# Block-causal attention with a gated linear unit on one core: the gated unit and its weights four steps later, output weights loaded over all partitions, the output tile ahead of the third score tile, fewer dummy matmuls

## The chip, the cores and the metric

The kernel runs on one core of a Trainium2 chip. The metric is the device time of one execution in microseconds (us). Every ratio below is the mean time of one kernel's fast runs over the mean of the other's fast runs of the same rounds, with a 95% interval; it is therefore not quite the ratio of the medians that stand beside it. A run is called slow when it is over 1.5% above the fastest of the same kernel; slow runs are left out of the ratios.

## The reference

Batch 8, 8 heads, 576 positions, head size 64; all inputs and outputs are float32.

```
scores = 0.125 * q @ k^T, masked so that block i (64 positions) sees blocks j <= i
x      = softmax(scores) @ v, heads side by side: [8, 576, 512]
gate   = sigmoid(causal depthwise convolution of x over 5 positions)
out    = (gate * (x @ w_val)) @ w_out
```

## The kernel before

A *step* handles one pair of heads: p = 0 to 31, four steps per batch element. The *gated unit* follows some steps behind. Its work for a quarter of a batch element, called a gated step here, is half a convolution (one of 80 small matmuls serves two gated steps), two value tiles and about one output tile. The engines are PE (matmuls), ACT (exp, tanh, copies), DVE (copies and products out of the matmul banks) and POOL (casts and masks); SP issues the loads. In the steps traced below each engine's instructions stand in the order in which the program emits them (after the change ACT's copy of the output tile starts at 119.84 us, the third exp, emitted behind it, at 120.32).

```python
# PSUM: two "S" tiles of two banks, used in turn; four "G" banks, used in turn.
psS = tile_pool(name="psS", bufs=2, ...)
GT  = [psG.tile([128, 512], fp32, ...) for i in range(4)]

def s_tile(p, t): ...      # matmuls into the next S tile, then exp on ACT out of it
def s_last(b): ...         # the last 64 positions' keys: the next S tile, then exp
def conv(b, hf): ...       # 80 matmuls into the next S tile and two G banks, then tanh x3 on ACT
def val(b, hf, x): ...     # 4 matmuls into a G bank, then DVE (needs the tanh)
def out_tile(u, t): ...    # 4 matmuls into a G bank, then a copy on ACT, then the store

wr = gbank()
for _ in range(9):                                   # dummy matmuls
    mm(wr[0:128, 0:512], wz[0:128, 0:128], wz[0:128])
cast_qk(0, first=True); trans(0)

def load_w_out(j):                                   # four loads, steps 3 and 4
    nc.sync.dma_start(
        out=w_st2[32 * j:32 * j + 32],
        in_=moe_w_out[128 * j:128 * j + 128].rearrange("(x a) n -> a x n", x=4))

for p in range(NP):
    loads(p)                       # QK tile of step p+4, V tile of step p+2, weights in steps 1 to 4
    s_tile(p, 0); s_tile(p, 1)
    weights(p)
    av(p - 1)
    trans(p + 2)                   # (from step 4 on; needs POOL's cast of that QK tile)
    s_tile(p, 2)
    mask(p); cast_v(p + 1); cast_qk(p + 3)           # POOL; the mask needs the third exp
    bq, m = divmod(p - 5, 4)
    if bq >= 0 and m % 2 == 0: conv(bq, m // 2)
    if p % 4 == 3: s_last((p + 1) // 4)
    xtrans(p - 1)
    out()
    if bq >= 0:
        for x in (0, 1): val(bq, m // 2, 2 * (m % 2) + x)
# ... cut: after the loop, five gated steps without attention work
```

`s_tile` computes scores and their exp, `av` multiplies them with V, `trans` and `xtrans` are transposes on PE (of Q and K, and of the attention's result x), `mask` and the casts to 16 bits run on POOL.

The softmax here doesn't subtract the row's maximum and nothing guards it: scores larger than these inputs give would overflow.

## Time and profile before

| | before |
|---|---|
| median of 4 runs, us | 206.47 (205.06 to 208.52) |
| span of the profiled run, us | 203.2 |
| PE busy | 183.9 us, 91% |
| ACT, DVE, POOL busy | 69%, 64%, 40% |

First the page of the kernel before: busy time by engine, then the span in 40 slices of 5.1 us (busy tenths of PE, granted clock in tenths, DMA busy tenths, GB/s). The granted clock is the share of its full clock that PE was allowed.

```profile
PE 183.9 (91%) x3681; PEld 128.5 (63%) x3681; DVE 129.1 (64%) x283; ACT 140.1 (69%) x190; POOL 82.0 (40%) x168
PE   3789867978999999999999999999999999889992
PEclk9966996699999999999999999999999999999999
DMA  5999999999496769686888769794888542113334
GB/s 148 260 266 292 296 283 180 198 240 236 119 279 184 221 194 269 196 228 174 234 231 233 216 192 264 228 243 114 234 254 247 161 118 85 58 56 108 135 129 155
```

PE looks busy from 50 us on and has holes and a lowered clock before. GB/s falls to 180 and 198 in the seventh and eighth slice, 30 to 41 us, while the DMA share stays at 9 tenths or more.

The same by stretches. The columns are the stretch and its length, then busy us and instruction counts of PE, its weight loads, DVE, ACT and POOL, then granted clock, DMA share (1.0 is 16 engines busy; it is above 1 where more than 16 packets overlap) and GB/s.

```profile
25.00:30.00 5.00, 3.69 (x79) 2.70 (x75) 3.65 (x8) 4.49 (x6) 3.10 (x6) 1.00 1.13 288
30.00:35.00 5.00, 3.91 (x59) 2.89 (x59) 4.36 (x11) 2.96 (x3) 1.41 (x5) 0.75 1.20 176
35.00:40.00 5.00, 4.02 (x107) 3.04 (x108) 2.15 (x3) 2.02 (x4) 1.48 (x3) 0.57 1.17 204
80.00:160.00 80.00, 78.62 (x1743) 56.19 (x1740) 56.17 (x122) 64.35 (x88) 35.59 (x68) 1.00 0.78 220
```

Up to about 50 us the loads set the pace: the DMA engines are full (share 1.13 to 1.20), PE is busy 3.7 to 4.0 of 5 us, and part of that at a lowered clock (0.75 and 0.57). From 80 to 160 us PE is busy 98% of the time and nothing else is.

The chain of waits says the same for the first part (start, duration, what):

```profile
24.41 7.29 DMA qks<-in_k_dram
31.71 8.15 DMA qks<-in_k_dram
39.87 6.47 DMA vs<-in_v_dram
46.78 0.60 POOL v L131
```

Now one steady step in the order of time (start, duration, engine, line, operation, operands). It begins with the first two score tiles at 111.20 us.

```profile
111.20 0.61 PE L33 MATMUL S<-qkT 64*128 64x512 f16 x6
111.41 1.05 POOL L126 CAST qk<-qks 128x1024 f16<-128x1024 f32 x1
111.69 3.04 ACT L185 ACTIVATE pt<-S 128x1024 f16<-128x1024 f32 x3 [0.78 <-PE S L33]
112.66 0.61 PE L151 MATMUL G<-ident,qk 128*128 128x128 f16 x8
113.21 0.28 PE L33 MATMUL S<-qkT 64*128 64x256 f16 x2
```

The three exps run without a gap (3.04 us). The POOL cast that the QK transposes need ends at 112.46, and the transposes start at 112.66: 0.2 us of slack. A step with a convolution takes about 5.7 to 6.0 us and one without 4.84.

### The profile page before, as it was taken

How to read it: one execution, taken by the hardware profiler on the slowest of the kernel's cores; microseconds unless marked ns; L12 is line 12 of the kernel's file. 1: busy time of each engine (PE TensorE's matmuls, PEld its weight loads, DVE VectorE, ACT ScalarE, POOL GpSimd, SP SyncE). 2: the span in 40 equal slices, each digit the busy share in tenths (PEclk: the TensorE clock that was granted, in tenths of full speed). 3: DMA queues.
4: the chain of work that ended last, by engine and by line, in shares of the span. 5: the costliest groups of instructions: out<-in, count | busy, mean ns of one | idle time of the engine just before them, and what ended most of it. 6: DMA issues, size and time to landing. Idle time of an engine off the chain costs nothing.

```text
span 203.2 us, 8654 instructions
## 1 busy us (share of the span) xinstructions
PE 183.9 (91%) x3681; PEld 128.5 (63%) x3681; DVE 129.1 (64%) x283; ACT 140.1 (69%) x190; POOL 82.0 (40%) x168
## 2 busy tenths in 40 slices
PE   3789867978999999999999999999999999889992
PEld 1367655656677676676676766676777766566650
DVE  4237878477576857686768576585768575536251
ACT  4165885457778787878787978778787878692621
POOL 7352953166445454545343534245454542210000
PEclk9966996699999999999999999999999999999999
DMA  5999999999496769686888769794888542113334
GB/s 148 260 266 292 296 283 180 198 240 236 119 279 184 221 194 269 196 228 174 234 231 233 216 192 264 228 243 114 234 254 247 161 118 85 58 56 108 135 129 155
DMA packets 70225, 40.43 MB, mean 199 GB/s; under 512 B 48165, under 2 KB 64549, under 8 KB 70186
## 3 DMA queue, kind: packets, MB, share of 16 engines
q1 hardware_dynamic: 69904, 39.60, 73.8%
q8 instruction: 29, 0.48, 1.1%
q10 hardware_dynamic: 282, 0.27, 0.4%
q14 instruction: 10, 0.08, 0.2%
HBM read 30.42 MB, written 9.44 MB: 196 GB/s over the span
## 4 chain that ended last, share of the span: by engine, by line
PE 59%; ACT 14%; DMA 11%; issue 7%; DVE 5%; POOL 2%; SPq 0%; ACTq 0%; POOLq 0%; DVEq 0%
PE G L33 39%; ACT pt L185 14%; PE S L33 11%; DMA qks<-in_k_dram 8%; PE G L241 5%; DMA vs<-in_v_dram 3%; PE G L151 3%; DVE x L232 3%; DVE rc L231 1%; POOL qk L126 1%; PE G L138 1%; DVE idfold L308 1%; DVE qk L157 0%; DVE osb L289 0%; DVE ident L303 0%
## 5 line engine op out<-in xcount | busy, mean ns | idle before, releaser
L185 ACT ACTIVATE pt<-S 128x1024 f16<-128x1024 f32 x96 | 94.2, 1022 | 35.6 <-PE S L33 33.6
L201 POOL MEMSET pt<- 64x384 f16 x32 | 13.2, 413 | 88.3 <-ACT pt L185 88.3
L277 DVE SCALAR_TENSOR_TENSOR gv<-th,G 128x288 f16<-128x288 f32 x64 | 28.4, 454 | 26.1 <-PE G L33 24.8
L162 DVE COPY qkT<-G 128x1024 f16<-128x1024 f16 x31 | 37.7, 1216 | 5.1 <-PE G L151 5.1
L33 PEld LDWEIGHTS <-pt 128*128 128x128 f16 x960 | 32.5, 100 | 7.3 <-issue 3.8
L33 PE MATMUL G<-xt,w_val 128*128 128x288 f16 x256 | 36.6, 286 | 0.0
L33 PE MATMUL G<-w_out,gv 128*128 128x512 f16 x144 | 36.5, 379 | 0.0
L33 PE MATMUL G<-v,pt 128*128 128x65 f16 x896 | 35.4, 197 | 0.2
L126 POOL CAST qk<-qks 128x1024 f16<-128x1024 f32 x31 | 32.4, 1045 | 3.4 <-DMA qks<-in_k_dram 3.3
L232 DVE TENSOR_TENSOR x<-G,rc 128x320 f16<-128x320 f32 x64 | 31.5, 492 | 2.2
L33 PEld LDWEIGHTS <-w_val 128*128 128x128 f16 x256 | 25.0, 98 | 11.8 <-issue 0.2
L291 ACT COPY osb<-G 128x512 f32<-128x512 f32 x34 | 20.0, 589 | 14.4 <-PE G L33 13.2
L33 PE MATMUL S<-qkT 64*128 64x512 f16 (+1 forms) x248 | 28.7, 308 | 0.3 <-ACT pt L185 0.2
L151 PE MATMUL G<-ident,qk 128*128 128x128 f16 x256 | 21.3, 231 | 5.3 <-POOL qk L126 5.3
L33 PEld LDWEIGHTS <-qkT 64*128 64x128 f16 x496 | 15.3, 95 | 14.7 <-issue 7.7
L231 DVE RECIPROCAL rc<-G 128x5 f32<-128x5 f32 x64 | 12.1, 189 | 16.9 <-PE G L33 16.5
L131 POOL CAST v<-vs 128x512 f16<-128x512 f32 x32 | 19.8, 618 | 5.8 <-DMA vs<-in_v_dram 4.4
L151 PEld LDWEIGHTS <-qk 128*128 128x128 f16 x256 | 16.2, 103 | 6.8 <-POOL qk L126 6.1
L243 DVE COPY xt<-G 128x576 f16<-128x576 f16 x32 | 14.5, 452 | 8.9 <-PE G L241 8.9
L33 PEld LDWEIGHTS <-gv 128*128 128x128 f16 x144 | 12.7, 98 | 10.1 <-DVE gv L277 0.5
L33 PE MATMUL S<-xt,DG 32*32 32x288 f16 x640 | 17.0, 295 | 1.3 <-ACT pt L185 0.5
L33 PE MATMUL G<-xt,DG 32*32 32x288 f16 x640 | 17.1, 296 | 0.0
(53 smaller groups left out, 141.7 us busy)
## 6 DMA issues: line engine op xcount, KB each, us to landing
out_dram<-osb SPq DMA_DIRECT2D x36, 256.0 KB, 2.2
qks<-in_q_dram SPq DMA_DIRECT2D x32, 256.0 KB, 4.2
vs<-in_v_dram SPq DMA_DIRECT2D x64, 128.0 KB, 4.4
qks<-in_k_dram SPq DMA_DIRECT2D x31, 256.0 KB, 4.6
tlst<-in_q_dram SPq DMA_DIRECT2D x8, 128.0 KB, 4.0
tlst<-in_k_dram SPq DMA_DIRECT2D x8, 128.0 KB, 4.6
vtst<-in_v_dram SPq DMA_DIRECT2D x8, 128.0 KB, 5.0
w_st<-in_moe_w_val_dram SPq DMA_DIRECT2D x2, 512.0 KB, 6.9
```

The source lines that it names most:

```text
L33: nc.tensor.matmul(out=out, lhsT=lhsT, rhs=rhs, start=start, stop=stop, skip_group_check=True)
L126: nc.gpsimd.tensor_copy(out=o, in_=s)
L131: nc.gpsimd.tensor_copy(out=v16s[p % NV][0:128, 0:4, 0:2, 0:64], in_=s)
L151: nc.tensor.transpose(out=r[:, o:o + 128], in_=t[0:128, c, 2 * i:2 * i + 2, 0:64], identity=ident16[0:128, 0:128])
L162: nc.vector.tensor_copy(out=o[0:128].rearrange("p i (s n) -> p i s n", n=4), in_=src)
L185: nc.scalar.activation(out=pts[p % NPT][0:128, 0:2, 512 * t:512 * t + 512], in_=s[0:128, 0:2, 0:512], func=AF.Exp, bias=0.0, scale=0.125)
L201: nc.gpsimd.memset(pt[64:128, 0:2, 0:1536].rearrange("p h (t s) -> p h t s", t=3)[:, :, :, 0:64], 0.0)
L231: nc.vector.reciprocal(out=rc[0:128], in_=O[:, :, 64:65])
L232: nc.vector.tensor_tensor(out=x[0:128, 0:5, h, 0:64], in0=O[:, :, 0:64], in1=rc[0:128].to_broadcast([128, 5, 64]), op=ALU.mult)
L243: nc.vector.tensor_copy(out=xts[b % NX][0:128, g, 4:4 + SEQ], in_=r[:, 0:SEQ])
L277: nc.vector.scalar_tensor_tensor(out=gv[u][0:128, x, bi, hf, 0:288], in0=t[0:128, x, 0:288], scalar=1.0, in1=r[0:128, 0:288], op0=ALU.add, ...
L291: nc.scalar.copy(out=o[0:128], in_=r[0:128, 0:512])
```

## The change

The intent: the loads of 2 MB of weights shall not compete with the loads of the first steps, so they and the gated unit come four steps later (the lag grows from five steps to nine); the output weights shall spread over all 128 partitions; fewer dummy matmuls stand ahead of the first real work; and the output tile gives PE something to do ahead of the third score tile.

The diff, cut to its core:

```diff
-    for _ in range(9):
-        mm(wr[0:128, 0:512], wz[0:128, 0:128], wz[0:128])
+    warm(4)
     cast_qk(0, first=True)
     trans(0)
+    warm(3)
...
-    def load_w_out(j):
+    def load_w_out(x):
         nc.sync.dma_start(
-            out=w_st2[32 * j:32 * j + 32],
-            in_=moe_w_out[128 * j:128 * j + 128].rearrange("(x a) n -> a x n", x=4))
+            out=w_st2[0:128, x],
+            in_=moe_w_out.rearrange("(j x a) n -> x j a n", j=4, x=4)[x])
... (value weights: loaded in steps 4, 5 for 1, 2; scaled in 7 to 10 for 4 to 6;
...  output weights: loaded in steps 6, 7 for 3, 4; cast in 9, 10 for 6, 7)
     for p in range(NP):
+        gs = p - 9
         loads(p); s_tile(p, 0); s_tile(p, 1); weights(p); av(p - 1)
         trans(p + 2)                      # from gs >= 0 on; at the end of the step before that
+        out()
+        if len(outs) > 2: out()
         s_tile(p, 2)
         mask(p); cast_v(p + 1); cast_qk(p + 3)
-        conv(...)                         # when due
         if p % 4 == 3: s_last((p + 1) // 4)
+        if gs >= 0 and gs % 2 == 0: conv(gs // 4, gs % 4 // 2)
         xtrans(p - 1)
-        out()
-        if len(outs) > 2: out()
         val(...), val(...)
... (after the loop nine gated steps for five; in the last two batch elements DVE copies every second output tile)
```

More of the change, by code (lines that the diff above doesn't have):

```diff
@@ L287, in out_tile @@
         o = p4.tile([128, 512], fp32, tag="osb", name="osb")
-        if u == B // 2 - 1 and t >= 6 and t % 2 == 0:
+        if u == B // 2 - 1 and t % 2 == 0:
             nc.vector.tensor_copy(out=o[0:128], in_=r[0:128, 0:512])
@@ L328, with warm @@
     wr = gbank()
-    for _ in range(9):
-        mm(wr[0:128, 0:512], wz[0:128, 0:128], wz[0:128])
+    def warm(n):
+        for _ in range(n):
+            mm(wr[0:128, 0:512], wz[0:128, 0:128], wz[0:128])
+    warm(4)
     cast_qk(0, first=True)
     trans(0)
+    warm(3)
     cast_tails(0, nc.vector)
@@ L366, in weights @@
                                     in1=convT[0:128].to_broadcast([128, 20, 32]), op=ALU.mult)
-        for x in {4: (0,), 5: (1,), 6: (2, 3)}.get(s, ()):
+        for x in {7: (0,), 8: (1,), 9: (2,), 10: (3,)}.get(s, ()):
             nc.vector.tensor_scalar(
@@ L372, in weights @@
                 scalar1=0.5, scalar2=None, op0=ALU.mult)
-        if s in (6, 7):
-            a = 2 * (s - 6)
+        if s in (9, 10):
+            a = 2 * (s - 9)
             nc.gpsimd.tensor_copy(out=w_out_sb[0:128, a:a + 2, 0:512],
@@ L387, in loads @@
             load_vtail(b + 1)
-        if p in (1, 2):
-            load_w_val(p - 1)
-        if p in (3, 4):
-            load_w_out(2 * p - 6)
-            load_w_out(2 * p - 5)
+        if p in (4, 5):
+            load_w_val(p - 4)
+        if p in (6, 7):
+            load_w_out(2 * p - 12)
+            load_w_out(2 * p - 11)
     outs = []
@@ L402, in out @@
             out_tile(*outs.pop(0))
+    LAG = 9
     for p in range(NP):
+        gs = p - LAG
         loads(p)
@@ L411 @@
             av(p - 1)
-        if 3 < p < NP - 2:
+        if gs >= 0 and p + 2 < NP:
             trans(p + 2)
@@ L415 @@
                 trans_tails((p + 2) // 4)
+        out()
+        if len(outs) > 2:
+            out()
         if p > 0:
@@ L426 @@
                 cast_tails((p + 3) // 4, nc.gpsimd)
-        if p < 4:
+        if p % 4 == 3 and p + 1 < NP:
+            s_last((p + 1) // 4)
+        if gs >= 0 and gs % 2 == 0:
+            conv(gs // 4, gs % 4 // 2)
+        if p > 0:
+            xtrans(p - 1)
+        if gs < 0:
             trans(p + 2)
@@ L430 @@
                 trans_tails((p + 2) // 4)
-        bq, m = divmod(p - 5, 4)
-        if bq >= 0 and m % 2 == 0:
-            conv(bq, m // 2)
-        if p % 4 == 3 and p + 1 < NP:
-            s_last((p + 1) // 4)
-        if p > 0:
-            xtrans(p - 1)
-        out()
-        if len(outs) > 2:
-            out()
-        if bq >= 0:
-            for x in (0, 1):
-                val(bq, m // 2, 2 * (m % 2) + x)
-            if m % 2 == 1:
-                complete(bq, m // 2)
-    b = B - 1
-    av(NP - 1)
-    out()
-    for x in (2, 3):
-        val(b - 1, 1, x)
-    complete(b - 1, 1)
-    xtrans(NP - 1)
-    out()
-    conv(b, 0)
-    out()
-    conv(b, 1)
-    out()
-    for hf in range(2):
-        for x in range(4):
-            val(b, hf, x)
-            out()
-        complete(b, hf)
+        else:
+            for x in (0, 1):
+                val(gs // 4, gs % 4 // 2, 2 * (gs % 2) + x)
+            if gs % 2 == 1:
+                complete(gs // 4, gs % 4 // 2)
+    av(NP - 1)
+    for gs in range(NP - LAG, NP):
+        b, hf = gs // 4, gs % 4 // 2
+        for x in (0, 1):
+            out()
+            val(b, hf, 2 * (gs % 2) + x)
+        if gs == NP - LAG:
+            xtrans(NP - 1)
+        if gs % 2 == 1:
+            complete(b, hf)
+            if gs + 1 < NP:
+                conv((gs + 1) // 4, (gs + 1) % 4 // 2)
     while outs:
```

## The prediction

> **What bounds the kernel now.** Two regimes. (a) To about 53 us the loads bound it: the chain of waits holds 22 us of landing loads between 24.4 and 46.3 us, the table by stretches shows PE busy only 3.6 to 4.4 of each 5 us with granted clock 0.57 to 0.75 in 30 to 40 us, and the DMA share is 1.1 to 1.2. Rate drops from about 290 to 180-200 GB/s at 30-41 us, when the four output-weight loads (256 KB each into 32 partitions, 7.5 to 9 us to landing) are in flight. [...] (b) From step 8 (53.1 us) PE bounds it: 98% busy; the 24 steps to 182.7 us take 5.40 us each (timeline: scores 0+1 0.54, AV 0.92, transposes 0.55, third scores 0.33, gated unit 2.6). The tail is dense too.
>
> **Early gains.** With four dummies, the first transposes start near 5.2 instead of 7.3 us: 2 us. Without weights in steps 1 to 4 [...], loads run at about 3.05 us per step (landings before), and step 10 starts near 50 us with 10 attention steps and one gated step done, against step 8 at 53.1 with three gated steps. A gated step costs PE about what an attention step costs (2.6 and 2.75 us), so the net gain is 4 to 6 us.
>
> **Steady losses.** In the trace exp of the third tile ends 3.5-3.75 us after a step's start. Ahead of it now stand the output matmuls (0.87) and their ACT copy (copy starts 1.07 after the first matmul, takes 0.5-0.6). So it ends near 4.6. Three things hang on it:
> 1. POOL: mask, V cast, QK cast follow that exp in 2.2 us plus 0.1; the next step's QK transposes wait for that cast and have only 0.2-0.4 us of slack. After the short (even) step they wait about 0.6-0.7 us, every second step.
> 2. Score ring of two buffers: in steps 11, 15, 19, 23, 27 the tail-score tile now precedes the conv, so conv takes the third tile's buffer and waits for its exp: about 1.1 us.
> 3. G ring of four banks: the second val tile reuses conv's first G bank, whose tanh follows exp: 0.2-0.4 us, as the output tile no longer stands between conv and val.
> Sum about 2.5-2.9 us per four steps beyond step 10, 12-15 us in all.
>
> **Sum.** 203.2 - 5 + 13 = 211 us of span; the timed run was 2.4 us over the span: 213.5 us, range 205 to 220. Faster by over 2%: 0.08; within 2%: 0.17; slower: 0.75.
>
> **What would show it.** First score matmul near 7.7 us instead of 9.8. DMA rate without the 180 GB/s trough. Gated step 0 starting near 45-48 us. PE busy share in 80-160 us down from 98% to about 87%; waits of the QK transposes on the POOL cast (none there now) in odd steps; score/conv matmuls waiting for the exp in every fourth step; val waiting for tanh. Steps near 6.0 us instead of 5.4.
>
> **What would make it wrong.** If the exp isn't delayed, the early gain wins: 199-202 us. [...]

I expected the output-weight loads to be faster over all partitions. The sum came to 203.2 - 5 + 13 = 211 us of span and 213.5 us of time: the 5 is the middle of the 4 to 6 us of early gain, an estimate of mine, and that these loads would be faster came from no trace.

## The result, and the profile after

| | before | after |
|---|---|---|
| median of 4 runs, us | 206.47 (205.06 to 208.52) | 227.14 (226.42 to 228.07) |
| ratio of the fast runs | | 1.103 (1.094 to 1.112) |
| span of the profiled run, us | 203.2 | 225.1 |
| PE busy | 91% | 83% |

The change makes the kernel 10.3% slower. I had predicted 3.8% slower (213.5 us) and a range that ends at 220. The direction was right, the size was not.

The page of the kernel after:

```profile
PE 186.4 (83%) x3679; PEld 126.5 (56%) x3679; DVE 132.5 (59%) x286; ACT 136.2 (60%) x187; POOL 82.9 (37%) x168
PE   3868977594377989878997989698987989999993
PEclk9959999769958999999999999999999999999999
DMA  5999989935894767666766667676773311134333
GB/s 156 273 266 285 215 232 337 219 107 156 211 262 128 210 188 210 188 189 190 209 174 162 193 196 199 195 185 191 238 204 106 93 50 49 49 119 157 115 134 143
```

The trough of 180 GB/s hasn't gone: it has moved to 45 to 56 us and deepened to 107 and 156 GB/s, and now the DMA share falls with it (3 and 5 tenths). The DMA engines are largely idle there (share 0.40 and 0.48). By stretches:

```profile
40.00:45.00 5.00, 2.94 (x31) 1.94 (x31) 3.19 (x7) 2.02 (x4) 1.84 (x4) 0.67 1.02 210
45.00:50.00 5.00, 4.72 (x82) 3.97 (x80) 3.82 (x8) 3.27 (x4) 2.37 (x5) 0.65 0.40 111
50.00:55.00 5.00, 1.94 (x100) 1.56 (x96) 2.51 (x7) 1.69 (x3) 2.58 (x3) 1.00 0.48 132
80.00:160.00 80.00, 70.43 (x1522) 47.76 (x1520) 50.18 (x108) 55.02 (x77) 32.03 (x61) 1.00 0.68 194
```

PE is busy 88% in the stretch where it was 98%. The chain of waits in the early part, and SP's issues there:

```profile
43.09 8.55 DMA vs<-in_v_dram
54.16 1.84 SPq L83
56.56 4.97 DMA vs<-in_v_dram
```

```profile
44.71 5.16 SPq L364 DMA_DIRECT2D w_st<-in_moe_w_out_dram  x2
49.91 0.87 SPq L92 DMA_DIRECT2D tlst<-in_q_dram  x1
51.56 2.56 SPq L83 DMA_DIRECT2D qks<-in_q_dram  x1
```

A V load that was issued at 43.09 landed 8.6 us later. That time alone shows little: in the kernel before, the V load between the two pairs of output-weight loads (issued at 34.19) took 7.61 us, and a K load 8.15 us. What is new is that SP was held 5.16 us by the issue of two output-weight loads, one of them 3.70 us (with the old form at the same place, in run e1 below, the longest took 1.94 us).

How many packets were in flight at each full microsecond, counted from the packet records of the two traces:

```
before, 30 to 42 us: 16 18 19 21 19 21 17 17 16 18 19 16 17
after,  44 to 56 us: 18  9 11  4  4  4  4  4 14 14  4 12 11
```

Four at each of five full microseconds. That number was the first lead. (The trace doesn't name the engine of a packet. The DMA share from 47 to 51 us is 0.27; four of 16 engines would be 0.25.)

A steady step after the change, the one that begins at 116.09 us (first score tiles at 116.09, then as shown):

```profile
117.22 1.05 POOL L126 CAST qk<-qks 128x1024 f16<-128x1024 f32 x1
118.32 0.62 PE L151 MATMUL G<-ident,qk 128*128 128x128 f16 x8 [0.59 <-POOL qk L126]
118.78 1.03 PE L33 MATMUL G<-w_out,gv 128*128 128x512 f16 x4
119.73 0.28 PE L33 MATMUL S<-qkT 64*128 64x256 f16 x2
119.84 0.58 ACT L291 COPY osb<-G 128x512 f32<-128x512 f32 x1 [1.31 <-PE G L33]
120.32 1.03 ACT L185 ACTIVATE pt<-S 128x1024 f16<-128x1024 f32 x1
121.40 0.29 PE L33 MATMUL S<-xt,DG 32*32 32x288 f16 x2 [1.15 <-ACT pt L185]
```

The bracket is the idle time of the engine before the instruction and what ended it. The third exp is no longer one of three in a row: it starts at 120.32, behind the output tile and its copy. The QK transposes wait 0.59 us for POOL's cast (which stands behind the mask of the step before, which needs that step's third exp), and the convolution waits 1.15 us for the third exp, whose S tile it must reuse. These are the waits of the prediction, with its sizes. The waits of both kernels from 100 to 180 us (total, times, longest), after:

```profile
PE G L151 <- POOL qk L126: 3.9, 6, 0.7
PE S L33 <- ACT pt L185: 3.5, 3, 1.2
PE G L33 <- ACT th L264: 0.8, 3, 0.3
```

The third line is the value tile's wait for tanh.

Before, there is no wait of L151 on POOL in that stretch, and one of this kind:

```profile
PE S L33 <- ACT pt L185: 0.5, 1, 0.5
```

Where the 21.9 us of span came from, by the start of the first exp of a step:

| step | before | after | |
|---|---|---|---|
| 8 | 53.8 | 44.6 | after is 9 us ahead, but with three gated steps fewer done |
| 10 | 64.0 | 57.5 | |
| 12 | 74.9 | 76.0 | four gated steps fewer done (3 for 7) |
| 31 | 177.8 | 189.6 | 19 steps: 5.42 us each before, 5.98 after |
| end | 203.2 | 225.1 | tail 25.4 before, 35.6 after |

The tail is 10.2 us longer for four more gated steps, which is their PE work (I had read 2.6 us for one). The steady steps lose 10.7 us from step 12 on, near the 12 to 15 us predicted from step 10 on. The rest, 1.1 us at step 12 with four gated steps owed, is the surprise: I had counted on being 4 to 6 us ahead on balance.

### The profile page after: what moved, and what is told of

The parts are those of the page before. It is cut to its first block, busy times and chain, and to the rows that moved or that the text cites. A ratio compares the mean times of both kernels' runs of the same rounds, so it can differ in the third digit from the quotient of the medians.

```text
span 225.1 us, 8654 instructions
## 1 busy us (share of the span) xinstructions
PE 186.4 (83%) x3679; PEld 126.5 (56%) x3679; DVE 132.5 (59%) x286; ACT 136.2 (60%) x187; POOL 82.9 (37%) x168
## 4 chain that ended last, share of the span: by engine, by line
PE 49%; DMA 19%; ACT 9%; POOL 8%; SPq 6%; issue 6%; DVE 0%; POOLq 0%; ACTq 0%; DVEq 0%
PE G L33 33%; PE S L33 9%; DMA vs<-in_v_dram 7%; DMA vtst<-in_v_dram 5%; PE G L151 5%; ACT pt L185 5%; DMA qks<-in_k_dram 5%; POOL qk L126 4%; SPq L83 3%; DMA tlst<-in_k_dram 3%; SPq L103 3%; POOL v L131 2%; PE G L241 2%; ACT th L264 2%; ACT th L261 1%
## 5 line engine op out<-in xcount | busy, mean ns | idle before, releaser
L33 PE MATMUL G<-xt,w_val 128*128 128x288 f16 x256 | 39.8, 291 | 2.6 <-ACT th L264 2.0
L277 DVE SCALAR_TENSOR_TENSOR gv<-th,G 128x288 f16<-128x288 f32 x64 | 29.0, 454 | 14.9 <-PE G L33 12.6
L291 ACT COPY osb<-G 128x512 f32<-128x512 f32 x31 | 18.1, 585 | 30.1 <-PE G L33 24.5
L126 POOL CAST qk<-qks 128x1024 f16<-128x1024 f32 x31 | 33.2, 1072 | 5.9 <-DMA qks<-in_k_dram 5.9
L151 PE MATMUL G<-ident,qk 128*128 128x128 f16 x256 | 21.7, 233 | 16.2 <-POOL qk L126 16.2
L33 PEld LDWEIGHTS <-w_val 128*128 128x128 f16 x256 | 24.5, 99 | 12.5 <-issue 4.9
L33 PE MATMUL S<-qkT 64*128 64x512 f16 (+1 forms) x248 | 29.4, 316 | 0.0
L151 PEld LDWEIGHTS <-qk 128*128 128x128 f16 x256 | 16.5, 104 | 18.5 <-POOL qk L126 17.9
L33 PE MATMUL S<-xt,DG 32*32 32x288 f16 x640 | 16.5, 287 | 5.8 <-ACT pt L185 5.8
L241 PE MATMUL G<-ident,x 128*128 128x128 f16 x160 | 15.3, 229 | 5.0 <-DVE x L232 5.0
L33 PEld LDWEIGHTS <-gv 128*128 128x128 f16 x144 | 12.7, 98 | 10.3 <-DVE gv L277 0.6
```

The costliest lines, as they stand in the source:

```text
L33: nc.tensor.matmul(out=out, lhsT=lhsT, rhs=rhs, start=start, stop=stop, skip_group_check=True)
L126: nc.gpsimd.tensor_copy(out=o, in_=s)
L151: nc.tensor.transpose(out=r[:, o:o + 128], in_=t[0:128, c, 2 * i:2 * i + 2, 0:64], identity=ident16[0:128, 0:128])
L241: nc.tensor.transpose(out=r[:, 128 * i:128 * i + 128], in_=x[0:128, i, 0:2, 0:64], identity=ident16[0:128, 0:128])
L277: nc.vector.scalar_tensor_tensor(out=gv[u][0:128, x, bi, hf, 0:288], in0=t[0:128, x, 0:288], scalar=1.0, in1=r[0:128, 0:288], op0=ALU.add, ...
L291: nc.scalar.copy(out=o[0:128], in_=r[0:128, 0:512])
```

## The experiments

Theory: three causes that add. (A) The new weight load keeps only four packets in flight, as many as its slowest source dimension has entries, and holds up the loads behind it. (B) The order inside the step delays the third exp and makes PE wait. (C) What is left is the lag. Rivals: the loads come at a bad place in the queue whatever their form; the steady loss stems from the lag or other load on DVE and POOL; a late scaling of the weights blocks DVE.

For (A): the new source pattern is j (4), a (32), n, and four packets were in flight. In the old one a (32) is the slowest dimension, and from 30 to 42 us, with the old loads under way, 16 to 21 were. Two counts don't show that the dimension sets the number; e1, e2 and e14 test it. I hadn't looked at it for the prediction.

### e1: the weight load as before

```diff
 # after, with
-            out=w_st2[0:128, x],
-            in_=moe_w_out.rearrange("(j x a) n -> x j a n", j=4, x=4)[x])
+            out=w_st2[32 * j:32 * j + 32],
+            in_=moe_w_out[128 * j:128 * j + 128].rearrange("(x a) n -> a x n", x=4))
```

> The kernel after the change, with one thing undone: the output weights load in four DMAs of 32 partitions each, as before. Theory A (the new pattern has 4 as its slowest source dimension [...]; 4 packets in flight at 47 to 51 us): the trough of 4 packets is gone, step 10 and 11 (8.2 and 11.1 us) fall to 5 to 7 us, time about 217 us (10 us less than 227). Rival B (the loads come at a bad place in the queue whatever their form, or the attention-only phase of nine steps starves): 225 us or more. Steps from 12 on stay near 6.0 us in either.

Measured: 222.78 us, 1.083 (1.077 to 1.090) of before, so 4.4 us less than after. The stretch of four packets is gone: from 45 to 56 us there are 235 GB/s at a DMA share of 1.18, for 133 at 0.48 in the kernel after. The theory's direction holds, but only 4 of the expected 10 us: step 10's first exp still starts at 56.8 us (57.5 after), with 15 to 21 packets in flight from 44 us on. The stretch of four packets held up the two steps that follow (step 12: 69.8 for 76.0), not the ones before. Some of what I had put down to (A) has another cause.

### e2: the kernel before with the new weight load alone

```diff
 # before, with load_w_out(x) of the change in place of load_w_out(j)
```

> The kernel before, with one thing changed: output weights loaded over all 128 partitions, as after the change. Theory A: 4 packets in flight for some 8 to 10 us, and the time is 6 to 12 us longer, about 214 us. The reading of my prediction [...]: 2 to 4 us shorter, about 203 us.

Measured: 211.02 us, 1.025 (1.019 to 1.032). The load alone costs 5 us, slightly under what theory A expected, and my prediction's reading of it as a gain is refuted.

### e3: the order inside the step as before

```diff
 # after, with
-        out(); if len(outs) > 2: out()
         if p > 0: s_tile(p, 2)
...
+        if gs >= 0 and gs % 2 == 0: conv(gs // 4, gs % 4 // 2)
         if p % 4 == 3 and p + 1 < NP: s_last((p + 1) // 4)
-        if gs >= 0 and gs % 2 == 0: conv(gs // 4, gs % 4 // 2)
         if p > 0: xtrans(p - 1)
+        out(); if len(outs) > 2: out()
```

> The kernel after the change, with the order inside a step as before: output tile after the x transposes, conv ahead of the last score tile; the new weight load stays. Theory (exp of the third tile delayed by the output tile; conv waiting for that exp's buffer): steps 12 to 31 fall from 5.98 to about 5.42 us, the waits of the transposes for POOL's cast go in that stretch, time about 216 to 217 us (10.6 us less). Rival (steady steps are slow because the gated unit is further behind, or DVE or POOL is loaded otherwise): 225 us or more.

Measured: 214.54 us, 1.041 (1.033 to 1.048): 12.6 us less than after. Steps 12 to 31 take 5.36 us each, so the lag doesn't slow the steady steps; the order does. It gives 2 us more than expected because the steps up to 12 gain too (first exp of step 12 at 72.9 us for 76.0).

### e4: only the dummy matmuls

```diff
 # before, with
-    nine dummies; cast_qk(0); trans(0)
+    warm(4); cast_qk(0); trans(0); warm(3)
```

> The kernel before, with only the dummy matmuls changed: four ahead of the first transposes and three behind them. First exp at 8.1 us instead of 10.2. If that carries through, 2 us shorter (204 us); if the loads set the pace of the first 50 us, under 1 us (206 us).

Measured: 207.02 us, 1.008 (1.000 to 1.016). The first exp starts at 8.06 us for 10.20, and nothing comes of it: step 3's is at 23.4 us (24.2 before) and step 8's at 55.2 (53.8). The loads set the pace there.

### e5: order and weight load as before, lag and dummies of the change

```diff
 # after, with the edits of e1 and e3
```

> The kernel after the change, with both the weight load's form and the order inside a step undone; what is left is the lag of nine steps with its later weights, the longer tail and the four plus three dummy matmuls. The two parts gave back 4.4 and 12.6 us of 227 alone; if they add, 210 us. My prediction's reading of the lag (4 to 6 us gained) would give 201 us; if the lag as such costs 3 to 4 us, 209 to 210 us.

Measured: 209.97 us, 1.013 (1.006 to 1.019). The parts add: undoing the load gives 4.4 us with the new order (e1) and 4.6 with the old one (e3 to e5), undoing the order gives 12.6 us with the new load (e3) and 12.8 with the old one (e1 to e5), and 3.4 us are left to e5. So what is left of the change is a loss, not the gain of the prediction. Where: step 12's first exp is at 70.6 us, 4.3 us ahead of the kernel before, with four gated steps fewer done, which cost PE about 10.4 us. The loads that bind have only moved: two stretches of e5,

```profile
40.00:45.00 5.00, 2.62 (x23) 1.72 (x23) 3.13 (x7) 1.47 (x3) 1.53 (x3) 0.62 1.00 202
50.00:55.00 5.00, 0.51 (x11) 0.39 (x8) 1.40 (x5) 0.98 (x2) 1.60 (x2) 0.98 0.89 182
```

PE is busy 0.5 of 5 us while the DMA share is 0.89.

### e6 and e7: the two places one at a time

```diff
 # e6: e1, with conv ahead of s_last again (out() stays ahead of the third score tile)
 # e7: e1, with out() behind xtrans again (conv stays behind s_last)
```

> As e1 (weight load as before), and in the step only the conv is put back ahead of the last score tile; the output tile stays ahead of the third score tile. By the mechanism of the prediction the wait of the conv for the third tile's exp (about 1.1 us in each of 5 steps with a last score tile) goes and the waits for POOL's cast and for tanh stay: steps 12 to 31 about 5.7 us instead of 5.98, time 217 to 218 us against 222.8 of e1. If the output tile's place does all the harm: 222 us. If the conv's place does: 212 us.

> As e1, and in the step only the output tile is put back behind the x transposes; the conv stays behind the last score tile. The conv still takes the third tile's buffer and waits for its exp in steps with a last score tile, about 1 us in each of 5 steps; the waits for POOL's cast and for tanh go. Against e1 (222.8) and e5 (210.0): 215 to 216 us. If the two places only harm together: 210 us.

Measured: e6 217.14 us, 1.052 (1.044 to 1.059), steps 12 to 31 at 5.75 us: as expected. e7 212.97 us, 1.041 (1.029 to 1.053), steps at 5.52 us: 2 to 3 us better than expected. Both places harm: from e1 with 1.083, putting back conv gives 3.2% and the output tile 4.2%, and both (e5) 7.0%. In e7 the conv's wait for the exp is left, at most 0.8 us for 1.2: with the output tile out of the way the third exp ends 3.0 to 3.3 us after the start of the step's first (steps 16 to 27), for 4.0 to 5.8 in e1.

```profile
PE S L33 <- ACT pt L185: 2.9, 4, 0.8
```

### e11: POOL's cast ahead of the mask

```diff
 # e1, from step 9 on
+            cast_qk(p + 3)
             mask(p); cast_v(p + 1)
-            cast_qk(p + 3)
```

> As e1 with both orders of the change kept, but from step 9 on POOL casts the next QK tile ahead of the mask, so that the cast no longer stands behind the delayed exp. If the wait of the QK transposes for that cast (0.6 to 0.7 us in every odd step) is on the critical path, about 11 steps give 7 us: 216 us; the conv's waits for the exp stay. If the transposes' wait only moves to the next one: 221 us or more.

Measured: 214.88 us, 1.046 (1.034 to 1.059), 7.9 us less than e1's 222.78; steps 12 to 31 take 5.58 us for 5.97. In the list of waits from 100 to 180 us the wait of the transposes on the cast is gone, and the convolution's is left as it was (3.5 us in 3 times, longest 1.2). So the wait of 0.6 to 0.7 us was on the critical path, and the delayed exp reached it through POOL's queue. (In the rounds of e7, e10, e11 and e12, three of seven runs of the kernel before were set aside as slow; against its median, 206.14 us, e7, e10 and e11 stand at 1.033, 1.025 and 1.042.)

### e8: the weights' scaling one step later

```diff
 # e5, with
-        for x in {7: (0,), 8: (1,), 9: (2,), 10: (3,)}.get(s, ()):
+        for x in {8: (0, 1), 9: (2,), 10: (3,)}.get(s, ()):
```

> As e5, but the first scaling of the value weights on DVE one step later (8 instead of 7). In the traces it waits 1.5 to 2.2 us for its load at the head of step 7, ahead of the normalisation of attention in DVE's queue, PE then idles and its clock halves from about 41 us on. If this wait is what the late weights cost, step 8 starts 3 to 5 us earlier and the time is 206 us or less; if PE is held there by the loads anyway, the same as e5 within 1 us.

Measured: 211.26 us, 1.020 (1.014 to 1.027). Step 8 does start 3.4 us earlier (first exp 41.2 for 44.6), and step 10 starts 1.0 us later (60.7 for 59.7). The wait of DVE was real and cost nothing: the next load would have held PE anyway. The rival falls.

### e10: the lag with early weights

```diff
 # e5, with weights loaded in steps 1 to 4 and scaled and cast in 4 to 7, as before the change
```

> As e5 (lag of nine, order and load form as before, four plus three dummies), but the weights are loaded and cast as early as before the change. It parts the lag from the weights' time. If the later weights cost the 3.4 us that e5 is behind: 206 to 207 us. If the lag itself costs (PE has only attention work while loads are short, and its gated work is done later): 210 us or more, as the bytes that step 9 needs are the same.

Measured: 211.26 us, 1.034 (1.022 to 1.045). With the weights where they were the loss stays. So it doesn't come from the weights' time.

### e13 and e16: the lag alone, and a smaller one

```diff
 # e13: e5, with nine dummies ahead of the first transposes
 # e16: e13, with LAG = 7 and the weights two steps earlier
```

> As e5, but with the nine dummy matmuls ahead of the first transposes as before: only the lag of nine steps, its later weights and the longer tail are left of the change. e5 is 3.4 us behind the kernel before, e4 (dummies alone) 1.0 us. If the two add, 208.8 us (2.4 behind). If the dummies are neutral and the lag does it all: 210 us.

> As e13 with a lag of seven steps and weights two steps earlier than with nine: a dose of the lag. If each step of lag while the loads bind leaves PE without its gated work, about half of e13's loss: 207.5 us, between the kernel before (206.3) and e13. If the lag as such is harmless: as before. If the loss stems from where the weights fall: as e13 or worse.

Measured, five rounds: e13 209.95 us, 1.022 (1.017 to 1.027); e16 206.84 us, 1.005 (0.999 to 1.012). The loss grows with the lag, by less than proportion for the first two steps of it (with seven it isn't clear of the noise). The runs show no gain from the dummies: without their change the lag costs 2.2%, with it (e5, another chip) 1.3%. The lag isn't quite alone in these runs: e5, e8, e10, e13 and e16 also keep the change's later place of the transposes in the steps before the first gated step, and its new tail. The tail of e5 is 10.3 us longer for four gated steps, no more than their PE work; the place of the transposes no run tests.

### e14: a slowest dimension of two

```diff
 # before, with each of the new loads split in two
+            out=w_st2[64 * f:64 * f + 64, x],
+            in_=moe_w_out.rearrange("(j x a) n -> x j a n", j=4, x=4)[x, 2 * f:2 * f + 2])
```

> The kernel before, with the output weights loaded in eight DMAs whose slowest source dimension is 2 (64 partitions each), a dose of the suspected cause. [...] 2 (or few) packets are in flight for a long stretch, and the loss is about double that of e2 (5 us with four): 10 us or more, 216 us or slower. If the form matters otherwise (partitions or packet size, the same here as in e2): 211 us.

Measured: 218.88 us, 1.066 (1.060 to 1.072), 13.1 us over before where e2 was 5.0. Packets in flight at each full microsecond from 36 to 48 us:

```
e14, 36 to 48 us: 3 2 3 2 16 17 20 4 13 2 2 2 2
```

Its stretches:

```profile
30.00:35.00 5.00, 4.03 (x54) 2.67 (x55) 4.33 (x9) 2.23 (x3) 2.17 (x4) 0.66 0.35 94
35.00:40.00 5.00, 4.00 (x126) 2.81 (x124) 3.50 (x8) 2.90 (x5) 1.67 (x4) 1.00 0.29 71
```

Two packets in flight at six of these 13 full microseconds, and three at two more, for a slowest source dimension of two; four at five in a row for a slowest dimension of four in the kernel after. In the thin stretches of both forms the number was that dimension, and the loss was larger with the smaller one (13.1 us for 5.0).

### e15: plain rows over all partitions, result wrong on purpose

```diff
 # before, with plain rows: slot x of partition p gets row 128 x + p
+        nc.sync.dma_start(out=w_st2[0:128, x], in_=moe_w_out[128 * x:128 * x + 128])
```

> The kernel before, with the output weights loaded as plain rows, 128 partitions per DMA, slowest dimension 128 on both sides; the rows then stand in the wrong partitions and the result is wrong on purpose. [...] My prediction's reading [...]: the trough of 180 to 200 GB/s goes, 2 to 3 us shorter, 203.5 us. [...]

Measured: 202.95 us, 0.990 (0.984 to 0.996). The trough goes:

```profile
30.00:35.00 5.00, 4.04 (x43) 2.62 (x44) 4.40 (x8) 2.18 (x3) 2.06 (x4) 0.53 1.00 246
35.00:40.00 5.00, 4.59 (x130) 3.67 (x128) 3.44 (x7) 2.96 (x5) 2.31 (x5) 0.79 1.14 311
```

246 and 311 GB/s stand where there were 176 and 204, at a DMA share of 1.00 and 1.14 (0.35 and 0.29 in e14). The gain that the change was after exists, about 2 to 3 us, with the load in this form. The partitions (128 for 32) and the order in which the source is read changed together, so which of them gives it isn't shown.

### e9, e12 and e17: attempts at a better kernel

```diff
 # e9:  before, with output weights loaded in steps 7, 8; output tiles from step 11 on
 # e12: before, with one quarter each in steps 9 to 12; output tiles from step 14 on
 # e17: before, with the plain-row load of e15 and 16 casts of 32 partitions by DVE, ACT and POOL
 #      in steps 5 to 8, which put the rows where they belong; output tiles from step 9 on
+                o = w_out_sb[32 * j:32 * j + 32, x, 0:512]
+                i = w_st2[32 * x:32 * x + 32, j, 0:512]
```

> The kernel before, with the output weights alone loaded later (steps 7 and 8, in the old form, pairs of quarters that lie in different halves of the partitions), cast in steps 10 and 11, and no output tile before step 11 (two per step then until the backlog is gone). The gated unit itself stays at its place, so PE keeps its work in the load-bound stretch. 1 MB less in the first 45 us is 3 to 4 us of loads at 285 GB/s: 202 us (2% less than 206). If the first stretch isn't bound by bytes: 206 us.

> The kernel before, with the output weights spread over steps 9 to 12 (one quarter each), cast in 13 and 14, output tiles from step 14 on, two per step until the backlog is gone. In e9 the loads saved up to step 8 (3.5 us) came back as waits in steps 10 to 13; here a quarter per step takes only the bandwidth that the missing output writes leave. Steps 9 to 14 then take 5.4 us on average and the saving stays: 203 us against 206.3. If the loads bind up to step 13 whatever is moved: 206 us.

> A version meant to beat both kernels: the kernel before, with the output weights loaded as plain rows [...] as in e15, and put into their partitions by 16 casts of 32 partitions in steps 5 to 8 (two on DVE, one on ACT, one on POOL per step) in place of two casts on POOL; output tiles from step 9. The result is right. If the casts fit into idle time: 203 to 204.5 us, 1% less than before. If they lengthen the load-bound steps, as before or slower.

Measured: e9 207.06 us, 1.000 (0.994 to 1.005); e12 205.99 us, 1.007 (0.994 to 1.019); e17 204.72 us, 0.999 (0.993 to 1.005), with a right result. None beats the kernel before by more than the noise. e12 is the instructive one: step 13's first exp is at 73.5 us for 79.7, but its output tiles were held back, and step 31's is at 177.7 for 177.8. Taking bytes out of the load-bound stretch also took out the PE work that hung on them.

## Why the prediction was wrong

What held:

- *The bounds.* Loads to about 53 us, PE after that: e4 shows the first (2.1 us gained at the first exp, none at the end), e3 the second.
- *"Steady losses ... 12-15 us in all."* Undoing the order gave 12.6 us (e3) and 12.8 (e1 to e5). By the profiled runs e3 gains 11.6 us in steps 12 to 31, a little under the range, and 3.1 us before step 12. The three waits were found with their sizes: transposes on the cast 0.59 and 0.7 us (predicted 0.6 to 0.7), convolution on the exp 1.15 (1.1), value tile on tanh up to 0.3 (0.2 to 0.4). Steps came out at 5.98 us ("near 6.0"), PE at 88% busy ("about 87%"). e6, e7 and e11 show each part by itself, the tanh wait excepted, which no run isolates.
- *The tail:* 10.2 us for four gated steps, dense.

What failed is the step "Early gains ... the net gain is 4 to 6 us". In its place stands a loss of 7.7 us (4.4 from after to e1, 3.4 from e5 to before, rounded), and the difference of 12 to 14 us is what the prediction was short of. It had three terms:

1. *"... loads run at about 3.05 us per step."* With the new load four packets were in flight at each full microsecond from 47 to 51 us, at a DMA share of 0.27. The sum had some 2 to 4 us of gain here (4 to 6 less the 2 of the third term) and the runs show 4.4 to 5.0 us of loss (e1, e2); e14 shows more of it (13.1 us lost with two packets in flight), e15 that a gain of 2 to 3 us comes with plain rows. I looked at the destination (which partitions) and not at the source's slowest dimension, which was the number of packets in flight in the thin stretches of both new forms (4 and 2).
2. *"Step 10 starts near 50 us."* It started at 57.0, and in e5, with the old load form, no earlier (first exp at 59.7). I took the rate of landings at the quietest place of the trace and applied it to a stretch that also had to carry 2 MB of weights and ran at a lowered clock in part (0.62 from 40 to 45 us and 0.70 from 45 to 50 in e5). From step 3 to step 7 e5 took 3.6 us a step, not 3.05.
3. *"The first transposes start near 5.2 instead of 7.3 us: 2 us."* They did, and it was worth nothing (e4), because the loads bind afterwards. The prediction says so of the stretch and still counted part of the gain.

Under the terms lies one idea that I had backwards. A gated step needs no loads except the weights, so it is the work that PE can do while the loads bind. Putting it nine steps behind leaves that stretch with attention work alone, and PE time that isn't used there is paid at the end. e13 and e10 show the cost: the lag costs 2.2%, and bringing the weights forward again doesn't help. That unused PE time is the reason is argued, from the balance of the traces, by first exps and ends: e5 is 4.3 us ahead of the kernel before at step 12, gains 1.0 us up to step 31 and pays 10.3 us more of tail, 5.0 us in all (span 208.2 for 203.2). e16 is 3.5 us ahead at step 12 and pays 5.6 us. So the first two steps of lag bring attention 3.5 us forward and the next two only 0.8 us, while each two cost about 5 us of tail. That is where the time went; that nothing else held PE back isn't shown.

Open: why the second two steps of lag bring so little forward. The granted clock was 0.62 from 40 to 45 us in e5, where PE was busy 2.62 of 5 us, but it fell in the kernel before as well (0.57 from 35 to 40 us), and over the span it is about the same (fast runs of e5 0.959 to 0.975, of the kernel before in the same rounds 0.966 and 0.967), so it doesn't look like the cause. What makes it fall isn't shown either. In the kernel before it was 0.50 from 32.50 to 39.33 us, and the longest gap of PE in the 4 us ahead was 1.22 us; in the kernel after, a gap of 3.06 us (50.39 to 53.45 us) was followed by 1.00 from 53.45 to 58.45 us. PE was busy 2.20 us of the 4 ahead of the fall in the kernel before, 3.31 of the 4 ahead of one in the kernel after (0.50 from 10.94 to 17.77 us), and 0.94 of the 4 that end with the gap.

## What to carry to other kernels

Before moving a load, read both of its access patterns: with 4 as the slowest dimension of the source, four packets were in flight here, and the steps behind came late (step 12 at 76.0 us for 69.8). In a stretch that loads bind, keep there the work that needs no loads; delaying it by four steps gave back less than it cost here (2.2% lost in e13). And when an instruction moves ahead of another on a busy engine, follow every queue that stands behind the second one: here one output tile of 0.9 us reached the transposes through ACT, a mask on POOL and a cast.
